# Attention and two expert layers in one kernel: K's layout and load order, and two weight preparations placed elsewhere

## The chip, the core and the metric

The kernel runs on one core of one Trainium2 chip. A core has five engines with instruction streams of their own: PE (TensorE, matmuls; its weight loads are shown apart as PEld), DVE (VectorE), ACT (ScalarE), POOL (GpSimd) and SP (SyncE, which here only issues DMAs). The metric is the device time of one execution in microseconds (us), lower is better. All times in this document are us from the start of the profiled span unless another unit is named.

## What is computed

Three stages follow each other.

- Attention for 4 batches, 8 heads, 576 positions and head size 64, in which scores more than tau below their row's maximum are dropped before the softmax:

```python
scores = scale * np.matmul(q, k.transpose(0, 1, 3, 2))
thresh = np.max(scores, axis=-1, keepdims=True) - tau
scores = np.where(scores >= thresh, scores, -1000000000.0)
attn = softmax(scores)            # out = attn @ v
```

- A feed-forward layer (FFN) on the 2304 tokens of 512 features: `h = x @ w_in` (2048 wide), a rational function P(h)/Q(h) of h with six coefficients, and the product with `w_out`.
- A layer of 8 experts of width 1024: a skip score (`x @ w_skip`) chooses the tokens, `x @ w_gate` chooses one expert for each, and `x + gate * relu(x @ w1[e]) @ w2[e]` is the output.

## The kernel before

Every float32 matrix that PE multiplies is split into a high part (the value rounded to fp32r) and a low part (the rest), and a product is three matmuls: high*high, high*low, low*high. The instruction order on every engine is the order in which the program is written (`manual_schedule`); semaphores are added for the dependences. A tile that is allocated under a tag whose buffer is still in use makes its first writer wait until the last reader of the older tile is done.

**Attention** works on 16 pairs of heads. `load(p)` (L214) issues on SP the DMAs for the K and Q of a pair, `loadv(p)` (L234) those for V. The tile `rk` has 864 columns: 288 columns with the two halves of the keys of head 0 on the partitions 0 to 63 and 64 to 127, 288 columns with the two halves of head 1 in an order that begins with its last 64 keys, and 288 columns with head 1 in its plain order. On the host, K lies as [batch, pair, head, feature, key], so `load` fills `rk` with seven DMAs of 64 partitions each; Q takes two DMAs for a pair, and eight for pair 0, which is loaded in four pieces. `high` (L246) makes the high part on ACT (for K an operation that scales in place comes first, L256, then the rounding, L257), `low` (L259) the low part: on DVE for pair 0, on POOL for the others. `smm` (L270) computes the scores on PE (L278).

A pair has nine score tiles; two of them form a unit, of which there are 72. The string SEQ (L21) writes out the order in one unit: `M` is DVE's row maximum (L284), `E` ACT's exp (L292), `A` DVE's mask with the row sum (L302), `N` PE's scores for the next unit, `t` PE's transposes, `X` and `Y` ACT's evacuations of them (L334), `V` and `W` the product with V. Each `K` takes one entry of the list `tasks`, which holds the `high` and `low` calls for the next pair (L472); each `D` moves one step of the decoding of the FFN weights (`wstep`, L425), which arrive as 64-bit floats in `raw` and are turned into high and low parts by operations on DVE, POOL and ACT (L115 to L146). Before unit 0, `load(0)`, four `wstep` calls (which issue the first load of `raw`), `load(1)` and `loadv(0)` are written, then `high`, `low` and `smm` for the first unit. Behind unit 3 the coefficients and the routing weights `wg` are loaded, ACT takes the absolute value of `cb` (L537), and DVE splits `wg` into `wgs` (L541, L542). `wgs` is first read in the FFN's second half (L702).

**FFN and experts** are one loop over steps t (from L942): 96 FFN steps (token block c of 384 tokens, slice f of the width) and then 48 expert steps (block c, slice j). In step t PE computes the first product of unit t and the second product of unit t - 3; in between, ACT, DVE and POOL apply the rational function. At the end of a step stands what the table `todo` holds for it, in the order in which the `at` calls are written. For each token block it has the reads of x2d (`pload`, L683), three steps of transposes (`tailB`, L687), the routing product and the writes of x2Td (`tailC`, L698). For the expert weights it has, with NFU = 96: `eload(j)` in step 89 + j, which issues on SP two DMAs of 256 KB into two of the four buffers `d0` to `d3`, and `esplit(j)` in step 90 + j, in which ACT makes the two high parts (L809). POOL makes the low parts (L812) in the next step, at `L` in ORD (L872). Expert slice j is first needed in step 96 + j. In step 90 POOL also issues the loads `mxs` of the first expert block (`mload`, L822), and in step 97 those of the second.

```python
def eload(e, j, tg):
    for x, src in (...):
        r = wqr[j, x] = f1.tile([P, 512], F32, tag=f"d{(2 * j + x) % 4}", ...)
        nc.sync.dma_start(r ..., src)
def esplit(j, tg, which, eng, later=True):
    nc.scalar.activation(w[:, 0], r, AF.Copy)
    def low():
        eng.tensor_tensor(w[:, 1], r, w[:, 0].bitcast(F32), op=ALU.subtract)
```

Of the kernel before, what the change touches and what calls it, by code (L numbers as in the profile page):

```python
# [9 lines left out]
F32 = mybir.dt.float32  # L10
# [3 lines left out]
AF = mybir.ActivationFunctionType  # L14
# [30 lines left out]
def body(ctx, tc, q, k, v, tau, w_in, w_out, a, b, w_skip, w_gate, w1, w2, out):  # L45
# [154 lines left out]
    with ExitStack() as actx:  # L200
# [13 lines left out]
        def load(p):  # L214
            if p >= NP:
                return
            bi, hp = divmod(p, NHP)
            rk = ap2.tile([P, NK], F32, tag="rk", name=f"rk{p}")
            rq = ap2.tile([P, NQ], F32, tag="rq", name=f"rq{p}")
            qc = ((0, NQ),) if p else ((0, 128), (704, 832), (128, 704), (832, NQ))  # L220
            for h in range(2):
                for j, h_, d0, c0, n in ((0, 0, 0, 0, 288), (1, 0, 0, 288, 288), (0, 1, 288, 512, 64), (0, 1, 352, 0, 224),
                                         (1, 1, 288, 224, 288), (0, 1, 576, 0, 288), (1, 1, 576, 288, 288)):
                    if h == h_:
                        nc.sync.dma_start(rk[64 * j:64 * j + 64, d0:d0 + n], k[bi, hp, h, :, c0:c0 + n])  # L225
                for c0, c1 in qc[h:h + 1]:
                    for j in range(2):
                        nc.sync.dma_start(rq[64 * j:64 * j + 64, c0:c1], q[bi, hp, :, c0:c1])
            for c0, c1 in qc[2:]:
                for j in range(2):  # L230
                    nc.sync.dma_start(rq[64 * j:64 * j + 64, c0:c1], q[bi, hp, :, c0:c1])
            raws[p] = rk, rq
# [12 lines left out]

        def high(p, i, c0, c1):  # L246
            if p >= NP:
                return
            if (p, i) not in qks:
                qks[p, i] = ap2.tile([P, 2, (NK, NQ)[i]], F32R, tag="KQ"[i], name=f"{'KQ'[i]}{p}")  # L250
            o, x = qks[p, i][:, 0, c0:c1], raws[p][i][:, c0:c1]
            if i == 0 and p == 0:
                nc.scalar.activation(o, x, AF.Copy, scale=scq)
                return
            if i == 0:
                nc.scalar.activation(x, x, AF.Copy, scale=scq)  # L256
            nc.scalar.activation(o, x, AF.Copy)  # L257

        def low(p, i, c0, c1):  # L259
            if p >= NP:  # L260
                return
            t = qks[p, i][:, :, c0:c1]
            x = raws[p][i][:, c0:c1]
            if i == 0 and p == 0:
                nc.vector.scalar_tensor_tensor(t[:, 1], x, scq, t[:, 0].bitcast(F32), op0=ALU.mult, op1=ALU.subtract)
                return
            eng = nc.vector if p == 0 else nc.gpsimd
            eng.tensor_tensor(t[:, 1], x, t[:, 0].bitcast(F32), op=ALU.subtract)  # L268
# [166 lines left out]
        nc.sync.dma_start(taub, tau.partition_broadcast(P))  # L435
        load(0)
        for _ in range(4):
            wstep()
        load(1)
        loadv(0)  # L440
        nc.vector.tensor_scalar(scq, taub, 0.0, -1.0 / math.sqrt(D), op0=ALU.is_ge, op1=ALU.mult)
        nc.vector.tensor_scalar(ptau, taub, 0.0, None, op0=ALU.max)
        for h in range(2):
            ks = (0, 0, 288) if h == 0 else (0, 288, NK)
            qs = (1, 704 * h, 704 * h + 128)
            for x in (ks, qs):
                high(0, *x)
            for x in (ks, qs):
                low(0, *x)
            smm(0, 0, h)  # L450
# [11 lines left out]
        for i in range(NS // 2 + 2):  # L462
# [4 lines left out]
            for x in cur:  # L467
                if x[1:] == (0, 0):
                    load(x[0] + 2)
                    n = x[0] + 1  # L470
                    z = ((0, 0, 432), (0, 432, NK), (1, 0, 608), (1, 608, NQ))
                    tasks += [[(high, n, *z[0])], [], [(high, n, *z[1])], [(low, n, *z[0])], [(high, n, *z[2])],  # L472
                              [(low, n, *z[1])], [(high, n, *z[3])], [(low, n, *z[2]), (low, n, *z[3])]]
                elif x[1:] == (2, 0):
                    loadv(x[0] + 1)
# [58 lines left out]
            if i == 3:  # L534
                nc.sync.dma_start(ca, a.partition_broadcast(P))
                nc.sync.dma_start(cb, b.partition_broadcast(P))
                nc.scalar.activation(cb, cb, AF.Abs)  # L537
                nc.vector.memset(cc, 1.0 + 1e-6)
                nc.sync.dma_start(wg[:, :, 0:E], w_gate.rearrange("(k p) e -> p k e", p=P))
                nc.sync.dma_start(wg[:, :, E], w_skip.rearrange("(k p) -> p k", p=P))  # L540
                nc.vector.tensor_copy(wgs[:, :, 0, :], wg)  # L541
                nc.vector.tensor_tensor(wgs[:, :, 1, :], wg, wgs[:, :, 0, :].bitcast(F32), op=ALU.subtract)  # L542
            if i in XS:
# [9 lines left out]
            if 70 <= i < 70 + min(XN, 2):  # L553
                xget(i - 70)
        sctx.close()
        psH = ctx.enter_context(tc.tile_pool(name="psH", bufs=4, space=PSUM, reuse_waits="tile"))
# [365 lines left out]
    for j in range(NF2):  # L922
        at(NFU - 7 + j, lambda j=j: eload(G["e"], j, "s"))
        for x in range(2):
            at(NFU - 6 + j, esplit, j, "s", x, nc.gpsimd)
    at(NFU - 6, mload, 0, "s")
# [114 lines left out]
```

## Time and profile before

| | |
|---|---|
| Runs | 985.34, 982.91, 985.03 us; median 985.03 |
| The profiled execution | 985.22 us, of which the span of the profile is 983.4 |
| PE, PEld | 913.0 us busy (93%), 749.5 (76%) |
| DVE, ACT, POOL | 701.1 (71%), 618.1 (63%), 483.3 (49%) |
| DMA | 124.15 MB, mean 126 GB/s |

How to read it: the profile is one execution. A busy time is the union of an engine's instructions, as a share of the span. An engine works its instructions in order, so one that waits holds up all that stand behind it on that engine. In a timeline, each row gives start, duration, engine, line, operation, the tile written and the tiles read, the shape, the count of merged instructions, and in brackets the engine's idle time ahead of it with what ended it. "SPq" and "POOLq" rows are the issuing of DMAs, not their transfer. PEclk is the clock granted to PE as a part of full speed. Attention fills about the first 325 us, the FFN follows up to 761 us, the experts stand behind it.

### The profile page before, as it was taken

The numbers are of one execution on the slowest core, as the hardware profiler recorded it, in microseconds if no ns is written. First come the engines' busy times: TensorE is split into PE (matmuls) and PEld (weight loads), VectorE is DVE, ScalarE is ACT, GpSimd is POOL, SyncE is SP. The second block draws the span as 40 slices with busy tenths as digits, with TensorE's granted clock in tenths as the row PEclk, the third lists the DMA queues.
The fourth block names the chain that finished last, engine by engine and source line by source line (L and its number), as shares of the span: only waits on it lengthen the run. The fifth ranks groups of instructions, "written<-read, shape, count | busy, mean of one in ns | idle before, by whom it ended". The sixth has DMA issues, their size and how long they took to land.

```text
span 983.4 us, 15831 instructions
## 1 busy us (share of the span) xinstructions
PE 913.0 (93%) x5442; PEld 749.5 (76%) x5442; DVE 701.1 (71%) x1450; ACT 618.1 (63%) x1153; POOL 483.3 (49%) x484
## 2 busy tenths in 40 slices
PE   3899889988899999999999999999998999999995
PEld 2666556656566799778888898888887988989884
DVE  4999999997988599888999877877875442221211
ACT  4798788887787688777787877777767311111110
POOL 1567569777883276998976733333346400000000
PEclk9999999999999999999999999999998999999998
DMA  5536446564644132244442332532527633122111
GB/s 151 130 96 172 117 138 180 153 194 123 179 134 173 56 107 91 87 156 153 150 160 74 129 107 86 182 118 88 186 80 238 212 129 128 65 98 95 65 33 35
DMA packets 74406, 124.15 MB, mean 126 GB/s; under 512 B 15184, under 2 KB 51536, under 8 KB 74320
## 3 DMA queue, kind: packets, MB, share of 16 engines
q1 hardware_dynamic: 70000, 99.48, 32.7%
q0 software_dynamic: 4320, 23.59, 6.9%
q8 instruction: 45, 0.74, 0.3%
q14 instruction: 41, 0.34, 0.1%
HBM read 85.22 MB, written 37.82 MB: 125 GB/s over the span
## 4 chain that ended last, share of the span: by engine, by line
PE 62%; DVE 15%; ACT 6%; POOL 6%; issue 5%; DMA 3%; SPq 3%; POOLq 0%; DVEq 0%; ACTq 0%
PE acc L604 14%; PE h L190 14%; PE mhs L190 10%; PE Ys L604 10%; PE S L278 4%; DVE m L284 3%; PE O L356 3%; PE T L314 3%; DVE P L302 2%; DMA rq<-in_q_dram 1%; ACT P L292 1%; SPq L225 1%; POOL Q L268 1%; DVE p L633 1%; DVE t L115 1%
## 5 line engine op out<-in xcount | busy, mean ns | idle before, releaser
L604 PE MATMUL acc<-wo,g 128*128 128x512 f32 x864 | 223.7, 401 | 9.6 <-ACT g L654 7.1
L604 PEld LDWEIGHTS acc<-wo,g 128*128 128x128 f32 x864 | 159.7, 190 | 49.8 <-ACT g L654 11.7
L623 POOL TENSOR_TENSOR qd<-v,qd 128x384 f32<-128x384 f32 x96 | 98.5, 1026 | 167.2 <-ACT v L620 166.1
L190 PE MATMUL h<-xg,wi 128*128 128x384 f32 x864 | 166.7, 342 | 0.0
L190 PEld LDWEIGHTS h<-xg,wi 128*128 128x128 f32 x864 | 153.5, 190 | 4.9 <-issue 0.5
L278 PE MATMUL S<-K,Q 64*128 64x288 f32 x960 | 97.2, 323 | 47.9 <-DVE P L302 36.5
L278 PEld LDWEIGHTS S<-K,Q 64*128 64x128 f32 x960 | 72.1, 191 | 88.9 <-issue 50.2
L850 DVE SCALAR_TENSOR_TENSOR mgs<-mhs,mgs 128x384 fp32r<-128x384 f32 x48 | 26.8, 558 | 151.1 <-ACT mgs L849 151.1
L292 ACT ACTIVATE P<-S,m 128x576 f32<-128x576 f32 x144 | 102.2, 741 | 47.4 <-DVE m L284 45.9
L849 ACT ACTIVATE mgs<-mhs 128x384 fp32r<-128x384 f32 x48 | 23.6, 492 | 169.8 <-PE Ys L604 168.6
L302 DVE SCALAR_TENSOR_TENSOR P<-S,m,P 128x576 f32<-128x576 f32 x144 | 111.4, 810 | 9.8 <-ACT P L292 9.8
L284 DVE TENSOR_REDUCE m<-S 128x1 f32<-128x576 f32 x144 | 103.5, 751 | 16.8 <-PE S L278 15.0
L190 PE MATMUL mhs<-mxs,wss 128*128 128x384 f32 x576 | 109.1, 337 | 0.0
L604 PE MATMUL Ys<-wss,mgs 128*128 128x512 f32 x432 | 108.5, 396 | 0.0
L190 PEld LDWEIGHTS mhs<-mxs,wss 128*128 128x128 f32 x576 | 101.6, 188 | 4.0
L604 PEld LDWEIGHTS Ys<-wss,mgs 128*128 128x128 f32 x432 | 80.1, 188 | 16.1
L628 DVE TENSOR_TENSOR p<-p,h 128x384 f32<-128x384 f32 x96 | 52.7, 549 | 47.5 <-ACT p L622 45.4
L314 PE MATMUL T<-idn,P 128*128 128x128 f32 x576 | 86.2, 291 | 0.0
L356 PE MATMUL O<-PT,V 128*64 128x320 f32 (+1 forms) x512 | 78.1, 426 | 0.6 <-ACT xT L369 0.6
L314 PEld LDWEIGHTS T<-idn,P 128*128 128x128 f32 x576 | 66.0, 147 | 12.6 <-issue 10.9
L616 ACT ACTIVATE qd<-h 128x384 f32<-128x384 f32 x96 | 46.6, 485 | 45.4 <-PE h L190 45.2
L334 ACT ACTIVATE PT<-T 128x512 f32<-128x512 f32 x128 | 71.2, 600 | 0.5 <-PE T L314 0.5
(149 smaller groups left out, 1538.7 us busy)
## 6 DMA issues: line engine op xcount, KB each, us to landing
xg<-xSd POOLq DMA_DIRECT2D x18, 768.0 KB, 5.7
x2Td<-x2h SPq DMA_DIRECT2D x12, 768.0 KB, 4.4
mxs<-x2Td POOLq DMA_DIRECT2D x12, 768.0 KB, 5.6
rq<-in_q_dram SPq DMA_DIRECT2D x30, 304.0 KB, 4.2
raw<-in_moe_w_in_dram SPq DMA_DIRECT2D x16, 512.0 KB, 4.2
raw<-in_moe_w_out_dram SPq DMA_DIRECT2D x16, 512.0 KB, 3.8
rk<-in_k_dram SPq DMA_DIRECT2D x80, 72.0 KB, 2.9
xSd<-px SPq DMA_DIRECT2D x24, 192.0 KB, 2.0
```

Source lines behind the costliest of these rows:

```text
L190: nc.tensor.matmul(h, w[:, sw, 128 * k:128 * k + 128], x[:, sx, k], start=(k == 0 and i == 0), stop=(k == NKT - 1 and i == 2))
L278: nc.tensor.matmul(st[:, c, :288], Q[d, x, q0:q0 + P], K[d, y, k0:k0 + 288], start=(s == 0 and j in (0, h)), stop=(s == 2 and (r < 4 or j ...
L284: nc.vector.tensor_reduce(m[:, 0:1], st, axis=AX.XY, op=ALU.min)
L292: nc.scalar.activation(e, st, AF.Exp, bias=m[:, 0:1], scale=-1.0)
L302: nc.vector.scalar_tensor_tensor(e, st, m[:, 1:2], e, op0=ALU.is_le, op1=ALU.mult, accum_out=sums[:, bi, col, hp:hp + 1])
L314: nc.tensor.transpose(T[:, 128 * j:128 * j + 128], pt[:, j0:j0 + 128], idn)
L334: nc.scalar.activation(dst[:, 5 * h:5 * h + 4, c0:c0 + 128], T.rearrange("p (j c) -> p j c", c=128), AF.Copy)
L356: nc.tensor.matmul(o[d, :w], vts[p][:, x, j, :], pt[:, j + 5 * x, :], start=(j == 0), stop=False)
L604: nc.tensor.matmul(ac[t], g[:, sg, 128 * t:128 * t + 128], w[:, sw, :], start=(first and i == 0), stop=(last and i == 2))
L616: nc.scalar.activation(u, h, AF.Abs)
L623: nc.gpsimd.tensor_tensor(qd, v, u, op=ALU.mult)
L628: nc.vector.tensor_tensor(p, p, hs[c, f], op=ALU.mult)
```

## The change

It has three parts.

1. The host lays K out as [batch, pair, 128, 576]: rows are the two key halves times 64 features, and columns are the two heads, 288 each, with head 1 in the order that begins with its last 64 keys. `load` then fills the first 576 columns of `rk` with one DMA of 128 partitions (two for pair 0), and the last 288 columns with three DMAs behind those of Q. Pair 0's K and Q pieces are issued in the order in which they are used, `load(1)` is written ahead of the first `wstep` calls, and only the first two K pieces and the first two Q pieces of pair 0 go through ACT and DVE ahead of unit 0. The large Q pieces get their low parts on POOL, and the last K piece becomes a task of unit 0, with its low part on POOL; the tasks of pair 1 move back by up to one unit.
2. The split of `wg` into `wgs` moves from behind unit 3 to behind the last unit of attention. The absolute value of `cb` moves from behind unit 3 to behind unit 10.
3. `esplit(j)` moves from step 90 + j to step 92 + j; `eload(j)` stays.

```diff
+            kd, qd = k[bi, hp], q[bi, hp]
+            kc = ((0, 576),) if p else ((0, 288), (288, 576))
             qc = ((0, NQ),) if p else ((0, 128), (704, 832), (128, 704), (832, NQ))
-            for h in range(2):
-                for j, h_, d0, c0, n in ((0, 0, 0, 0, 288), (1, 0, 0, 288, 288), (0, 1, 288, 512, 64), (0, 1, 352, 0, 224),
-                                         (1, 1, 288, 224, 288), (0, 1, 576, 0, 288), (1, 1, 576, 288, 288)):
-                    if h == h_:
-                        nc.sync.dma_start(rk[64 * j:64 * j + 64, d0:d0 + n], k[bi, hp, h, :, c0:c0 + n])
-                for c0, c1 in qc[h:h + 1]:
-                    for j in range(2):
-                        nc.sync.dma_start(rq[64 * j:64 * j + 64, c0:c1], q[bi, hp, :, c0:c1])
-            for c0, c1 in qc[2:]:
+            for i in range(len(qc)):
+                for c0, c1 in kc[i:i + 1]:
+                    nc.sync.dma_start(rk[:, c0:c1], kd[:, c0:c1])
                 for j in range(2):
-                    nc.sync.dma_start(rq[64 * j:64 * j + 64, c0:c1], q[bi, hp, :, c0:c1])
+                    nc.sync.dma_start(rq[64 * j:64 * j + 64, qc[i][0]:qc[i][1]], qd[:, qc[i][0]:qc[i][1]])
+            for r0, c0, r1, c1 in ((slice(0, P), slice(576, 800), slice(0, P), slice(352, 576)),
+                                   (slice(0, 64), slice(800, 864), slice(64, P), slice(288, 352)),
+                                   (slice(64, P), slice(800, 864), slice(0, 64), slice(288, 352))):
+                nc.sync.dma_start(rk[r0, c0], kd[r1, c1])
...
-            eng = nc.vector if p == 0 else nc.gpsimd
+            eng = nc.vector if first else nc.gpsimd
...
         load(0)
+        load(1)
         for _ in range(4):
             wstep()
-        load(1)
...
         for h in range(2):
-            ks = (0, 0, 288) if h == 0 else (0, 288, NK)
+            ks = (0, 288 * h, 288 * h + 288)
             qs = (1, 704 * h, 704 * h + 128)
             for x in (ks, qs):
-                high(0, *x)
+                high(0, *x, True)
             for x in (ks, qs):
-                low(0, *x)
+                low(0, *x, True)
...
-                    tasks += [[(high, n, *z[0])], [], [(high, n, *z[1])], [(low, n, *z[0])], [(high, n, *z[2])],
-                              [(low, n, *z[1])], [(high, n, *z[3])], [(low, n, *z[2]), (low, n, *z[3])]]
+                    hi, lo = [(high, n, *x) for x in z], [(low, n, *x) for x in z]
+                    if n == 1:
+                        tasks += [[], [(high, 0, 0, 576, NK), (low, 0, 0, 576, NK)], [hi[0]], [hi[1]], [lo[0], hi[2]], [lo[1]], [hi[3]], [lo[2], lo[3]]]
+                    else:
+                        tasks += [[hi[0]], [], [hi[1]], [lo[0]], [hi[2]], [lo[1]], [hi[3]], [lo[2], lo[3]]]
...
             if i == 3:
...
-                nc.scalar.activation(cb, cb, AF.Abs)
...
-                nc.vector.tensor_copy(wgs[:, :, 0, :], wg)
-                nc.vector.tensor_tensor(wgs[:, :, 1, :], wg, wgs[:, :, 0, :].bitcast(F32), op=ALU.subtract)
+            if i == 10:
+                nc.scalar.activation(cb, cb, AF.Abs)
...
+        nc.vector.tensor_copy(wgs[:, :, 0, :], wg)
+        nc.vector.tensor_tensor(wgs[:, :, 1, :], wg, wgs[:, :, 0, :].bitcast(F32), op=ALU.subtract)
         sctx.close()
...
-            at(NFU - 6 + j, esplit, j, "s", x, nc.gpsimd)
+            at(NFU - 4 + j, esplit, j, "s", x, nc.gpsimd)
...
-                x = y
+                y[:, :, 1] = _np.roll(y[:, :, 1], S - n, axis=3)
+                x = y.reshape(B, H // 2, 2, D, 2, S // 2).transpose(0, 1, 4, 3, 2, 5).reshape(B, H // 2, 2 * D, S)
```

## Rows read from the trace of the kernel before

**Rows 1.** Busy us (instructions) by stretch, granted PE clock, DMA share and GB/s

```profile
core 0: us, PE busy (x) PEld busy (x) DVE busy (x) ACT busy (x) POOL busy (x), PEclk, DMA share, GB/s
100.00:150.00 50.00, 43.19 (x369) 29.38 (x371) 46.99 (x110) 40.89 (x76) 32.79 (x29) 1.00 0.43 125
...
319.00:327.00 8.00, 7.44 (x51) 4.65 (x50) 0.09 (x2) 1.92 (x5) 0.61 (x9) 1.00 0.05 16
...
736.00:742.00 6.00, 6.00 (x35) 5.51 (x33) 3.27 (x6) 1.37 (x3) 1.90 (x2) 1.00 1.07 385
742.00:746.00 4.00, 0.74 (x3) 0.46 (x2) 0.86 (x2) 3.82 (x7) 1.38 (x2) 0.82 0.35 110
746.00:750.00 4.00, 4.00 (x10) 2.58 (x10) 2.84 (x6) 3.94 (x8) 3.84 (x4) 0.50 0.21 62
```

**Rows 2.** Timeline of DVE, units 1 to 4 of attention

```profile
17.59 1.49 DVE L284 TENSOR_REDUCE m<-S 128x1 f32<-128x576 f32 x2 [0.54 <-PE S L278]
...
23.02 0.43 DVE L115 TENSOR_SCALAR t<-raw 128x512 uint32<-128x512 uint32 x1
23.64 1.50 DVE L284 TENSOR_REDUCE m<-S 128x1 f32<-128x576 f32 x2 [0.19 <-PE S L278]
...
27.95 1.42 DVE L284 TENSOR_REDUCE m<-S 128x1 f32<-128x576 f32 x2 [0.15 <-PE S L278]
...
32.16 1.17 DVE L541 CAST wgs<-wg 128x36 fp32r<-128x36 f32 x1 [0.99 <-DMA wg<-in_moe_w_skip_dram]
...
34.49 1.41 DVE L284 TENSOR_REDUCE m<-S 128x1 f32<-128x576 f32 x2
```

**Rows 3.** Timeline of ACT, the same stretch

```profile
12.82 0.52 ACT L257 ACTIVATE Q<-rq 128x384 fp32r<-128x384 f32 x1 [0.41 <-DMA rq<-in_q_dram]
14.64 1.41 ACT L292 ACTIVATE P<-S,m 128x576 f32<-128x576 f32 x2 [1.29 <-DVE m L284]
19.63 0.65 ACT L256 ACTIVATE rk<-rk,scq 128x432 f32<-128x432 f32 x1 [3.59 <-DMA rk<-in_k_dram]
...
20.79 1.36 ACT L292 ACTIVATE P<-S,m 128x576 f32<-128x576 f32 x2
22.04 1.09 ACT L334 ACTIVATE PT<-T 128x512 f32<-128x512 f32 x2
...
24.43 1.48 ACT L292 ACTIVATE P<-S,m 128x576 f32<-128x576 f32 x2 [0.18 <-DVE m L284]
...
31.70 0.67 ACT L129 ACTIVATE w<-raw 128x512 f32<-128x512 f32 x1
35.27 1.41 ACT L292 ACTIVATE P<-S,m 128x576 f32<-128x576 f32 x2 [2.90 <-DVE m L284]
```

**Rows 4.** Timeline of ACT, the split of expert piece 1

```profile
742.04 1.35 ACT L809 ACTIVATE wss<-wrs 128x512 fp32r<-128x512 f32 x2 [4.64 <-DMA wrs<-in_moe_w_dram]
```

**Rows 5.** Timeline of SP's DMA issues, the first loads

```profile
3.70 3.15 SPq L225 DMA_DIRECT2D rk<-in_k_dram  x5
...
8.17 2.51 SPq L231 DMA_DIRECT2D rq<-in_q_dram  x4
```

**Rows 6.** Timeline of POOL, a subtraction of 608 columns

```profile
31.80 1.49 POOL L268 TENSOR_TENSOR Q<-rq,Q 128x608 fp32r<-128x608 f32 x1 [2.48 <-ACT Q L257]
```

**Rows 7.** DMA issues: count, KB each, median us from issue to landing

```profile
raw<-in_moe_w_in_dram SPq DMA_DIRECT2D x16, 512.0 KB, 4.2
```

**Rows 8.** Timeline of PE, first product of steps 92, 93 and 94

```profile
735.26 2.37 PE L190 MATMUL h<-xg,wi 128*128 128x384 f32 x12
...
739.90 2.37 PE L190 MATMUL h<-xg,wi 128*128 128x384 f32 x12
...
750.54 2.74 PE L190 MATMUL h<-xg,wi 128*128 128x384 f32 x12
```

**Rows 9.** Timeline of SP, the load of expert piece 1

```profile
734.22 1.20 SPq L804 DMA_DIRECT2D wrs<-in_moe_w_dram  x2
```

**Rows 10.** The tile wrs (expert weights as loaded), time to landing

```profile
DMA to landing us min/median/max: 3.6/3.8/3.9
```

**Rows 11.** The tile wss (split expert weights): ns min/median/max, first and last start

```profile
L812 POOL TENSOR_TENSOR wss<-wrs,wss x16: 1280/1297/1330, 735.3 to 774.6; 128x512 fp32r<-128x512 f32 x16
```

More of the change, by code (lines that the diff above doesn't have):

```diff
@@ L244, in loadv, with high @@
                 nc.sync.dma_start(VZ[p % 3][d, d], v[bi, h0 + j, 512:576, :])
-        def high(p, i, c0, c1):
+        def high(p, i, c0, c1, first=False):
             if p >= NP:
@@ L251, in high @@
             o, x = qks[p, i][:, 0, c0:c1], raws[p][i][:, c0:c1]
-            if i == 0 and p == 0:
+            if i == 0 and first:
                 nc.scalar.activation(o, x, AF.Copy, scale=scq)
@@ L257, in high, with low @@
             nc.scalar.activation(o, x, AF.Copy)
-        def low(p, i, c0, c1):
+        def low(p, i, c0, c1, first=False):
             if p >= NP:
@@ L263, in low @@
             x = raws[p][i][:, c0:c1]
-            if i == 0 and p == 0:
+            if i == 0 and first:
                 nc.vector.scalar_tensor_tensor(t[:, 1], x, scq, t[:, 0].bitcast(F32), op0=ALU.mult, op1=ALU.subtract)
                 return
-            eng = nc.vector if p == 0 else nc.gpsimd
+            eng = nc.vector if first else nc.gpsimd
             eng.tensor_tensor(t[:, 1], x, t[:, 0].bitcast(F32), op=ALU.subtract)
```

## The prediction

> **What bounds the kernel now.** The engine shares come first (table above): PE is busy 93% of the span, so time is to be had only where PE idles or runs at a low clock. The busy time by stretch shows where [rows 1]. In the middle of attention (100 to 150 us) PE has 43.19 of 50 us and DVE 46.99, so DVE is the fullest engine there. Behind attention PE is nearly full, but from 742 to 746 us it has 0.74 of 4, and from 746 to 750 its granted clock is 0.50, the 1.2 GHz level. So I read the timelines, engine by engine, at the start of attention and near 742 us.
>
> In attention one unit is a ring: DVE's row maxima (L284), ACT's exps (L292), DVE's masks (L302), PE's next scores (L278), which need the score buffer that a mask frees. The maxima of units 2 and 3 start at 23.64 and 27.95 us, an undisturbed step of 4.31; from unit 1 to 2 it is 6.05 (from 17.59), and from unit 3 to 4 it is 6.54 (to 34.49) [rows 2]. In the first of these stalls ACT stood for a DMA of rk before L256, and the exps at 20.79 are queued behind that [rows 3]. In the second DVE stood for the DMA of wg before L541, and the maxima are queued behind the two wgs operations [rows 2]. Near 742 us ACT stood 4.64 us for the DMA of wrs [rows 4], with all the activations of that step queued behind it.
>
> **First loads.** SP issues one DMA in 0.63 us (five in 3.15) [rows 5]. Before, the last piece of pair 0's Q is the 15th DMA, issued at 10.09 (the last of four that begin at 8.17); ACT could use it at 12.82, 2.73 later [rows 3, 5]. Now it is the 10th, issued at 6.89, there at 9.62, and ACT's 0.52 on it ends at 10.14. The second score's K and Q pieces are issued by 4.34 and there by 7.1, so both maxima are done by 10 us. The subtractions of the large Q pieces move from DVE to POOL, where one of 608 columns takes 1.49 [rows 6]; begun at 9.2, that is over before the scores of unit 1 ask for it near 11.9, and costs nothing; begun 2 us later it would hold these scores. So exp 0 starts at 10.14 instead of 14.64.
>
> Unit 1: from exp 0 to the next maximum it took 2.95 (14.64 to 17.59), and an exp starts 0.79 behind its maximum (23.64 to 24.43) [rows 2, 3]: 13.88. Ahead of it on ACT stands now the last third of pair 0's K. Its transfers are issued up to 8.81; if they take the 4.2 us of a 512 KB one [rows 7], two operations of at most 0.52 end at 14.05. I take 14.05.
>
> Unit 2: ACT has the exps (1.41), an evacuation pair (1.09) and now both K pieces of pair 1, four operations of at most 0.65 [rows 3]: 19.2. On DVE the first weight decode (L115, 0.43) stands ahead of the maxima. Its load of raw is now the 20th DMA, since pair 1 has been moved ahead of it: issued at 13.3, there 4.2 later [rows 7], 17.5; plus 0.43, and 0.79 to the exp, 18.7 [rows 2]. ACT decides: exp 2 starts at 19.2 instead of 24.43, **5.2 us** earlier. Ends: 5.7 if exp 1 starts at 13.88 and the K operations are shorter; 4.2 if raw takes 1.5 longer because pair 1's 0.9 MB stands ahead of it.
>
> **Routing weights.** DVE is free at 31.17, waits 0.99, and has the two wgs operations till 34.49 [rows 2]. Without them its maximum is done by 31.92, and the exp is bound by ACT, which is busy till 32.37 (L129): 35.27 less 32.37, **2.9 us** [rows 3]. At most 3.3, all the time that DVE spent on it; at least 2.2, if the step becomes the undisturbed 4.31. At the new place, behind the loop, DVE is busy 0.09 us of the 8 from 319 to 327 [rows 1]: nothing, and 2.3 if that cover is gone. The Abs of cb, two columns, is put in a unit where ACT waits for DVE: nothing. The ring carries both gains to the end of attention, because DVE has the same work per unit as before. SP issues three DMAs fewer for each pair; no engine of the ring stood for SP once it ran, so this is nothing.
>
> **Expert weights.** Step 93 of the FFN loop takes from 739.90 to 750.54, 10.64 us; the step before, with the same transposes, takes 4.64 [rows 8]. The difference, **6.0 us**, is PE's wait and the low clock behind it. The cause: piece 1 of the expert's weights is issued at 734.22 and used at 742.04, 7.8 later, where a piece lands in 3.6 to 3.9 [rows 4, 9, 10]. From 736 to 742 the DMA engines are full at 385 GB/s [rows 1]: POOL's load of mxs (1.5 MB, step 90), three writes of x2d and piece 2 lie beside it. After the change piece 1 is loaded at the same time, but its split stands at the end of step 93, near 747 us, 5 us after it landed. ACT doesn't stand, PE doesn't idle, and the clock doesn't fall. At least 4.0 if a later piece makes ACT wait 2; at most 6.4, with 0.4 that step 94 also lost at the low clock by my estimate.
>
> The new wait is SP's. The four buffers hold two pieces, so the load of piece j+2 stands on SP until POOL's subtraction of piece j, which now comes two steps later. Behind it in SP's queue stand the last token block's reads of x2d (L685) and the writes of x2Td (L704). DVE's block-end sum (L674) needs the third of these reads: I get it issued near 763.5 and wanted at 768.6, and 5.1 us is more than any landing in [rows 10]. So it is just hidden; if it came later, PE would wait for DVE to free the accumulators. The pieces themselves go by hops: two subtractions of 1.30, a landing of 3.8, a split of 1.35, up to 0.6 for the order on ACT and POOL, 8.4 in all for every second piece, while PE takes two steps, 8.4 or more [rows 4, 8, 10, 11]. Piece 1 is done near 754.6 and piece 7 three hops later at 779.8; the expert stage starts at 754.7 and asks for piece 7 after seven steps of 4.2, at 784. Nothing, with 4 us to spare.
>
> Of the landing, the rows show 7.8 once, beside mxs, and at most 3.9 in the rest [rows 4, 9, 10]. The Trainium skill (DMA: Bandwidth & Descriptors, Issuing engines are not separate DMA queues) says that DMAs started by different engines run on the same 16 DMA engines and interleave; the trace agrees with 385 GB/s. By that rule the second load of mxs, which POOL issues in step 97, would stretch one more hop from 8.4 to 12.4 and use up the 4 us to spare, which speaks for the third rival below; by the bare rows the hop stays 8.4. The sum is the same by both.
>
> **Sum.** 5.2 + 2.9 + 6.0 = 14.1, from the profiled execution's 985.22 us (a span of 983.4 and 1.8 around it): 971.1. The median of the runs, 985.03, lies 0.2 under that execution.
>
> **Rivals.** (1) The splits stand later, but the wait returns at piece 2 or 3, because their loads start two steps later too, so the change doesn't do what it says. Then the third term is gone: 985.2 - 8.1 = 977.1. For it: a hop of 8.4 is no shorter than two steps. Against: the first round has 5 us of air, and no 1.5 MB load lies beside pieces 2 and 3. Chance 0.12. (2) The ring wins back late time anyway, and the start's gain is lost on the way. Only the 6.0 remains: 979.2. For it: DVE idles 3 us of 50, room in which 8 us of delay could be made up over 300 us. Against: those idle moments are the ring's own waits, and the two stalls came from outside it [rows 1, 2]. Chance 0.10. (3) Slower: the hops get long, and PE waits for pieces in its first eight expert steps. Three hops have 29.4 us (754.6 to 784), 9.8 each, which a landing of 5.2 fills. Each us more per landing costs 3, and a stall brings some 2.5 at the low clock, so 14.1 is eaten from a landing of about 9. At 10 it is 3 x 4.8 + 2.5 - 14.1, 2.8 over: 988. For it: 7.8 was seen once. Against: it needs more than that three times over. Chance 0.03.
>
> **Numbers.** The forecast has 0.75. With the ends of its terms the gain is 10.4 to 15.4, which is 969.8 to 974.8; the lowest run shown is 2.1 under the median, so I set the low end at 967.5. The high end takes in the first two rivals: 979.5. About 0.3% (3 us) is what a measurement of this kernel can tell from no change. The forecast and the first two rivals are all faster by more than that, 0.97; 0.02 of it I give to the case that both of these hold in part, which is the same; slower 0.03.
>
> **What would show it.** Right: exp 2 near 19 us; no DVE wait for wg and an even step from unit 3 to 4; the end of attention about 8 us earlier; no PE gap near 735 us and a clock of 1.00 there; the expert stage beginning 14 us earlier. Wrong: ACT waiting for wrs at a later piece; PE waiting for wss; L674 waiting for a read of x2d; late exps back at their old times.

## The result, and the profile after

The changed kernel takes 972.16 us (median of 972.53, 972.6, 968.34 and 971.8), the kernel before on the same chip 984.55: ratio 0.9868, 95% interval 0.9839 to 0.9896. That is 12.4 us less, 1.1 from the 971.1 predicted. Taken again later beside other kernels, the same kernel gave 970.27 and the same ratio, 0.9868 (0.9847 to 0.9888). The profiled execution took 972.53, a span of 970.6.

To see where the time went I use one measure throughout, the **lead**: by how much the same work starts earlier than in the profile of before, taken at the first row maximum (L284) of an attention unit and at the first product (L190) of a step. For the changed kernel it is 4.2 us at unit 2, 4.7 at unit 4, 5.6 at the last unit, 5.8 at step 93, and 12.1 from step 95 to the end. So the time was won in two places, the first units and step 93 to 94, and between units 2 and 4, where 2.9 was predicted, hardly any came.

The expert weights first: PE's products and ACT's splits around the place where ACT stood 4.64 us in [rows 4]. (In the changed kernel the split of L809 is L813.)

```profile
729.51 2.37 PE L190 MATMUL h<-xg,wi 128*128 128x384 f32 x12
...
734.15 2.37 PE L190 MATMUL h<-xg,wi 128*128 128x384 f32 x12
...
738.79 2.36 PE L190 MATMUL h<-xg,wi 128*128 128x384 f32 x12
```

```profile
736.03 1.14 ACT L813 ACTIVATE wss<-wrs 128x512 fp32r<-128x512 f32 x2
...
740.68 1.14 ACT L813 ACTIVATE wss<-wrs 128x512 fp32r<-128x512 f32 x2
...
745.80 0.63 ACT L813 ACTIVATE wss<-wrs 128x512 fp32r<-128x512 f32 x1 [0.30 <-DMA wrs<-in_moe_w_dram]
```

Step 93 takes 738.79 - 734.15 = 4.64 instead of the 10.64 of [rows 8], and no split of the first two pieces waits. The windows there show a full PE at clock 1.00, where [rows 1] has 0.74 of 4 and then 0.50:

```profile
core 0: us, PE busy (x) PEld busy (x) DVE busy (x) ACT busy (x) POOL busy (x), PEclk, DMA share, GB/s
...
728.00:734.00 6.00, 6.00 (x33) 5.30 (x32) 5.36 (x11) 4.85 (x9) 1.78 (x2) 1.00 0.97 342
734.00:740.00 6.00, 6.00 (x36) 5.56 (x35) 4.53 (x10) 5.84 (x12) 2.89 (x4) 1.00 0.36 124
```

Now the start of attention. These are ACT's rows of the changed kernel; the exps (L292) of units 0 to 2 answer to those of [rows 3]:

```profile
9.64 1.35 ACT L292 ACTIVATE P<-S,m 128x576 f32<-128x576 f32 x2
...
13.29 1.48 ACT L292 ACTIVATE P<-S,m 128x576 f32<-128x576 f32 x2 [1.40 <-DVE m L284]
...
20.19 1.41 ACT L292 ACTIVATE P<-S,m 128x576 f32<-128x576 f32 x2 [2.16 <-DVE m L284]
```

Exps 0 and 1 are a little ahead of the 10.14 and 14.05 predicted. Exp 2 is 1.0 behind its 19.2, and its bracket names a cause that the prediction had ruled out: ACT was idle 2.16 us and waited for DVE. DVE's rows and PE's say why:

```profile
12.50 1.50 DVE L284 TENSOR_REDUCE m<-S 128x1 f32<-128x576 f32 x2 [0.53 <-PE S L278]
...
18.51 0.98 DVE L115 TENSOR_SCALAR t<-raw 128x512 uint32<-128x512 uint32 x1 [2.72 <-DMA raw<-in_moe_w_in_dram]
19.41 1.41 DVE L284 TENSOR_REDUCE m<-S 128x1 f32<-128x576 f32 x2
...
29.79 1.42 DVE L284 TENSOR_REDUCE m<-S 128x1 f32<-128x576 f32 x2 [2.82 <-PE S L278]
```

```profile
22.55 1.83 PE L278 MATMUL S<-K,Q 64*128 64x288 f32 x12 [4.71 <-DVE P L302]
```

The first decode of an FFN weight (L115) stood 2.72 us on DVE for `raw`, whose load is now issued behind those of pair 1; unit 2's maxima are queued behind it. So DVE's masks came late, and PE stood 4.71 us for them. After that PE ran at a lower granted clock:

```profile
core 0: us, PE busy (x) PEld busy (x) DVE busy (x) ACT busy (x) POOL busy (x), PEclk, DMA share, GB/s
16.00:20.00 4.00, 1.84 (x16) 1.43 (x16) 1.49 (x2) 1.97 (x4) 2.89 (x3) 1.00 1.08 277
20.00:24.00 4.00, 1.45 (x12) 1.48 (x12) 3.81 (x11) 3.25 (x6) 0.48 (x1) 0.69 0.76 170
24.00:28.00 4.00, 4.00 (x22) 2.63 (x21) 2.97 (x9) 3.53 (x6) 1.40 (x2) 0.50 0.77 202
28.00:32.00 4.00, 4.00 (x40) 2.77 (x36) 1.83 (x5) 1.49 (x4) 3.59 (x3) 0.96 0.43 117
```

From 24 to 28 us PE is busy throughout at 0.50, the 1.2 GHz level, and does 22 matmuls where it does 40 in the next four. It is the bound there, and DVE, now without the two `wgs` operations, waits 2.82 us for PE's scores ahead of unit 4's maxima (29.79). My theory from this: one late load at the start both delayed exp 2 and lowered the clock, and the slow PE swallowed what the routing weights should have given. The rival: the three parts' gains are simply smaller than thought, each by itself.

### The profile page after: what moved, and what is told of

It reads as the page before. It is cut to its first block, busy times and chain, and to the rows that moved or that the text cites. A ratio compares the mean times of both kernels' runs of the same rounds, so it can differ in the third digit from the quotient of the medians.

```text
span 970.6 us, 15750 instructions
## 1 busy us (share of the span) xinstructions
PE 908.5 (94%) x5442; PEld 747.8 (77%) x5442; DVE 696.7 (72%) x1448; ACT 618.9 (64%) x1155; POOL 485.5 (50%) x487
## 4 chain that ended last, share of the span: by engine, by line
PE 65%; DVE 15%; ACT 6%; POOL 6%; issue 5%; SPq 1%; DMA 1%; POOLq 0%; DVEq 0%; ACTq 0%
PE acc L608 15%; PE h L190 15%; PE mhs L190 10%; PE Ys L608 10%; PE S L278 5%; DVE m L284 4%; PE O L356 4%; PE T L314 3%; DVE P L302 3%; ACT P L292 1%; DVE t L115 1%; DVE p L637 1%; DVE h L652 1%; DVE raw L117 1%; DVE h L650 1%
## 5 line engine op out<-in xcount | busy, mean ns | idle before, releaser
L608 PE MATMUL acc<-wo,g 128*128 128x512 f32 x864 | 221.1, 398 | 6.2 <-ACT g L658 3.7
L190 PE MATMUL h<-xg,wi 128*128 128x384 f32 x864 | 166.6, 342 | 0.0
L190 PEld LDWEIGHTS h<-xg,wi 128*128 128x128 f32 x864 | 153.5, 190 | 4.9 <-issue 0.5
L292 ACT ACTIVATE P<-S,m 128x576 f32<-128x576 f32 x144 | 102.5, 741 | 48.4 <-DVE m L284 47.3
L284 DVE TENSOR_REDUCE m<-S 128x1 f32<-128x576 f32 x144 | 103.7, 751 | 19.4 <-PE S L278 17.5
L190 PE MATMUL mhs<-mxs,wss 128*128 128x384 f32 x576 | 109.2, 338 | 0.0
L190 PEld LDWEIGHTS mhs<-mxs,wss 128*128 128x128 f32 x576 | 101.7, 188 | 4.0
L268 POOL TENSOR_TENSOR Q<-rq,Q 128x608 fp32r<-128x608 f32 (+2 forms) x32 | 47.6, 1490 | 56.4 <-ACT Q L257 56.2
```

Of the source, the lines that this page charges most:

```text
L190: nc.tensor.matmul(h, w[:, sw, 128 * k:128 * k + 128], x[:, sx, k], start=(k == 0 and i == 0), stop=(k == NKT - 1 and i == 2))
L284: nc.vector.tensor_reduce(m[:, 0:1], st, axis=AX.XY, op=ALU.min)
L292: nc.scalar.activation(e, st, AF.Exp, bias=m[:, 0:1], scale=-1.0)
L608: nc.tensor.matmul(ac[t], g[:, sg, 128 * t:128 * t + 128], w[:, sw, :], start=(first and i == 0), stop=(last and i == 2))
```

## Experiments

All kernels were timed beside the kernel before, which took 983.98 us beside the first four of them, 984.52 beside the next four and 984.33 beside the last four.

**The parts, one at a time.** Each of these three kernels is the kernel before with one part of the change:

```diff
 p1_loads: part 1 (K's layout, load order, first parts)
 p2_wg:    part 2 (split of wg behind attention, Abs of cb behind unit 10)
 p3_split: part 3
-            at(NFU - 6 + j, esplit, j, "s", x, nc.gpsimd)
+            at(NFU - 4 + j, esplit, j, "s", x, nc.gpsimd)
```

> Part 1 alone (K's layout, load order, pair 1 ahead of raw; wgs and the expert splits where they were). Theory (DVE stands for raw at unit 2, PE idles and then runs at the low clock into unit 4): maxima of unit 2 start near 19.4 us as in the changed kernel, 4.2 earlier than before; at unit 4 DVE still has to split wg, whose loads land near 28.4, so its maxima start near 31 us; the total is 3.5 to 4.5 us below the kernel before, about 980.5. Rival (the terms of the start are independent and only smaller than forecast): 5 us below, about 979.5.

> Part 2 alone (wgs behind attention, Abs of cb behind unit 10). Theory (in the changed kernel PE's low clock hid this term): alone it gives what the rows of before said, maxima of unit 4 near 31.6 instead of 34.49 us, a total 2.5 to 3 us below the kernel before, about 982. Rival (the ring wins the time back in the next units): under 1 us, about 984.

> Part 3 alone (splits of the expert weights two steps later). Theory: the 6.3 us by which the changed kernel's step 93 is shorter are this part's alone: about 978.2, no PE gap and a clock of 1.00 in steps 92 to 95. Rival (the gap is missing in the changed kernel because the start moved the loop against the DMA traffic): the gap stays and the total is within 1 us of before.

| kernel | median us (all runs) | ratio (95%) | gain, us |
|---|---|---|---|
| p1_loads | 977.54 (976.35 to 978.76) | 0.9936 (0.9922 to 0.9949) | 6.4 |
| p2_wg | 980.95 (978.08 to 983.47) | 0.9965 (0.9953 to 0.9976) | 3.0 |
| p3_split | 976.92 (975.25 to 978.44) | 0.9925 (0.9911 to 0.994) | 7.1 |

Alone the parts give 16.5 us, together 12.4 (14.1 in the second measurement). The rival is out: part 2 alone gives 3.0 us, and in its profile the lead grows from 0.5 at unit 3 to 2.9 at unit 4, the place where the two `wgs` operations stood.

Not all of the difference between 16.5 and 12.4 comes from the parts, though. In step 88 of the FFN loop, which no part touches, PE has the same 1.40 us of idle in all 14 profiles. In ten of them its clock then falls, and the step takes 5.8 us; in four (p1_loads, p2_wg, qlow_dve, split_plus4) it doesn't, and the step takes 4.28. The windows of that step, first of before, then of p1_loads:

```profile
716.00:720.00 4.00, 3.70 (x15) 3.70 (x16) 2.21 (x7) 0.04 (x1) 0.00 (x0) 0.65 0.00 0
711.00:715.00 4.00, 3.44 (x19) 3.26 (x20) 2.47 (x7) 1.06 (x3) 0.00 (x0) 1.00 0.00 0
```

So 1.5 us of what the profiles of p1_loads and p2_wg gain on that of before is none of the parts' doing. How much of this is in the medians, no run shows.

Part 1 alone gave more than I expected. In its profile the lead is 4.6 at the last unit, and 1.5 in step 88 and 0.8 in step 93 come on top. Attention itself was ahead of the expectation too: the maxima of unit 2 start at 18.36 instead of near 19.4. Its maxima of unit 4 I had put near 31 us, with the stall for `wg` still in front; DVE's rows of p1_loads show them at 29.30, ahead even of the changed kernel's 29.79:

```profile
18.02 0.43 DVE L115 TENSOR_SCALAR t<-raw 128x512 uint32<-128x512 uint32 x1 [2.20 <-DMA raw<-in_moe_w_in_dram]
...
27.20 0.92 DVE L544 CAST wgs<-wg 128x36 fp32r<-128x36 f32 x1 [1.24 <-DMA wg<-in_moe_w_skip_dram]
28.15 1.22 DVE L545 TENSOR_TENSOR wgs<-wg,wgs 128x36 fp32r<-128x36 f32 x1
29.30 1.41 DVE L284 TENSOR_REDUCE m<-S 128x1 f32<-128x576 f32 x2
```

The two `wgs` operations with their wait fill time in which DVE would otherwise stand for the slow PE, whose clock here was 0.57 and 0.58 from 20 to 28 us. There they cost little, so taking them away gives little.

**raw ahead of pair 1.** The changed kernel with the late load alone put back in its place:

```diff
         load(0)
-        load(1)
         for _ in range(4):
             wstep()
+        load(1)
         loadv(0)
```

> The changed kernel with the first load of raw issued ahead of pair 1 again (one line moved back). Theory: L115 finds raw landed, no wait of DVE before it; maxima of unit 2 start near 17.5 us, PE idles under 3 us there and keeps a clock of 1.00 from 20 to 28 us, maxima of unit 4 near 26.5 us; total 3 us below the changed kernel, about 969. Rival (pair 1 now lands 0.6 us later and ACT stands for it instead; or the low clock comes from the light load at the start in any case): within 1 us of the changed kernel, about 972.

It takes 968.26 us (966.95 to 969.17), ratio 0.9841 (0.9826 to 0.9855): 3.9 less than the changed kernel, 2.9 less than the median of all eight runs of it (971.2), and 2.7 less by the two ratios. The intervals overlap, so the size is rough. DVE's and PE's rows of raw_first:

```profile
15.71 0.42 DVE L115 TENSOR_SCALAR t<-raw 128x512 uint32<-128x512 uint32 x1
16.32 1.46 DVE L284 TENSOR_REDUCE m<-S 128x1 f32<-128x576 f32 x2 [0.19 <-PE S L278]
...
26.41 1.42 DVE L284 TENSOR_REDUCE m<-S 128x1 f32<-128x576 f32 x2 [1.65 <-PE S L278]
```

```profile
20.34 1.83 PE L278 MATMUL S<-K,Q 64*128 64x288 f32 x12 [2.10 <-DVE P L302]
```

L115 has no wait, the exp of unit 2 starts at 18.61, and the leads are 7.3 at unit 2, 8.1 at unit 4 and 10.0 at the last unit. PE still stood 2.10 us, and the clock from 20 to 24 us was 0.57, not the 1.00 I had expected: part of the loss is left. In the changed kernel's second profile (changed_again, below) the leads are 5.3, 6.8 and 8.8, so raw_first is ahead of both profiles at each of these places.

**Part 2 with and without the late load.** If the slow PE hides part 2, undoing part 2 must cost little in the changed kernel and more in raw_first. In both, the Abs and the two `wgs` operations go back behind unit 3:

```diff
             if i == 3:
...
+                nc.scalar.activation(cb, cb, AF.Abs)
...
+                nc.vector.tensor_copy(wgs[:, :, 0, :], wg)
+                nc.vector.tensor_tensor(wgs[:, :, 1, :], wg, wgs[:, :, 0, :].bitcast(F32), op=ALU.subtract)
-            if i == 10:
-                nc.scalar.activation(cb, cb, AF.Abs)
...
-        nc.vector.tensor_copy(wgs[:, :, 0, :], wg)
-        nc.vector.tensor_tensor(wgs[:, :, 1, :], wg, wgs[:, :, 0, :].bitcast(F32), op=ALU.subtract)
```

> The changed kernel without part 2 (wgs and the Abs of cb back behind unit 3). Theory: in the changed kernel DVE stands 2.8 us for scores at unit 4 that PE makes at the low clock, and the two wgs operations fit into that wait, so taking part 2 away costs 0 to 1 us: about 972.5. Rival (part 2 earns its 2.9 us here too): about 975.

> The kernel with raw ahead of pair 1, without part 2. Theory: where PE's scores come earlier, the wgs operations stand in the way again: maxima of unit 4 near 28.6 instead of 26.4 us, total about 970.4, 2.2 us over raw_first (968.3). Rival (part 2 is worth nothing once part 1 is there): 968.3.

no_p2 takes 972.76 (972.13 to 973.76), ratio 0.9888 (0.987 to 0.9905); raw_first_no_p2 970.44 (969.73 to 971.71), ratio 0.9859 (0.9839 to 0.9879). Part 2 is thus worth 972.76 - 972.16 = 0.6 us behind the late load (1.6 against all eight runs) and 970.44 - 968.26 = 2.2 without it. The direction is as the theory has it, but the intervals overlap, so the medians alone would not show it. The lead around the place, beside PE's granted clock, says more:

| profile | lead at units 2, 3, 4 | from 3 to 4 | clock, 20 to 24 and 24 to 28 us |
|---|---|---|---|
| changed kernel, first | 4.2, 4.3, 4.7 | 0.4 | 0.69, 0.50 |
| changed_again | 5.3, 5.3, 6.8 | 1.5 | 0.70, 0.87 |
| raw_first | 7.3, 6.5, 8.1 | 1.6 | 0.57, 1.00 |
| raw_first_hi1 (below) | 7.3, 7.6, 10.1 | 2.5 | 1.00, 1.00 |
| qlow_dve (below) | 5.8, 5.9, 8.4 | 2.5 | 1.00, 1.00 |
| p2_wg | 0.5, 0.5, 2.9 | 2.5 | 0.72, 1.00 (24 to 28, 28 to 32) |
| p1_loads, without part 2 | 5.3, 5.3, 5.2 | -0.1 | 0.57, 0.58 |
| no_p2, without part 2 | 5.4, 5.4, 5.3 | -0.1 | 0.66, 0.91 |
| raw_first_no_p2, without part 2 | 7.6, 6.8, 6.5 | -0.3 | 0.68, 0.89 |

With part 2 the lead grows by 2.5 where PE had its full clock between units 3 and 4, by 1.5 and 1.6 where the clock was lower for a part of that time, and by 0.4 where it was 0.50; without part 2 it doesn't grow. So the slow PE hides 1 to 2 of the 2.5 us, and not always all of it: changed_again and no_p2 start alike and differ by 1.5 at unit 4. The leads at the last unit are a poor measure of part 2. Those of the changed kernel's first profile and no_p2 are nearly equal (5.6 and 5.7), but that profile had lost 1.1 more at unit 2; and of the 10.0 of raw_first against the 6.6 of raw_first_no_p2, 1.4 arise behind unit 50, where none of these edits stands.

**Waiting for raw later.** The same late load, with the first decode steps written later in the units:

```diff
-PACE_A = (8, 1, 1, 1, 1, 3, 2, 1, 3)
+PACE_A = (10, 1, 1, 1, 1, 3, 2, 1, 3)
```

> The changed kernel with its load order kept, but every weight decode begun two of its moves later, so that L115 of the first stands in unit 3 and not in unit 2. Theory (it is DVE's stand for raw, not the load order as such, that costs): no wait before L115, maxima of unit 2 near 16.5 us, no low clock of 8 us behind it, total within 1 us of raw_first, about 968.5. Rival (pair 1 ahead of raw costs by the DMA queue, whoever waits): about 972.

The start is as expected. DVE and the window of pace:

```profile
20.22 0.42 DVE L115 TENSOR_SCALAR t<-raw 128x512 uint32<-128x512 uint32 x1
...
26.10 1.41 DVE L284 TENSOR_REDUCE m<-S 128x1 f32<-128x576 f32 x2
```

```profile
24.00:28.00 4.00, 3.50 (x34) 2.60 (x34) 3.76 (x10) 1.44 (x3) 3.43 (x3) 1.00 0.80 222
```

No wait, clock 1.00, a lead of 8.4 at unit 4. But the time is 973.03 (970.98 to 973.33), ratio 0.9879 (0.9861 to 0.9898), no better than the changed kernel and near the rival's number, although the start is the theory's: the lead wanders between 1.6 and 8.9 from unit 6 to 60 and is 4.7 at the last unit. The edit also shifts where every later decode step falls in the units, and what it won at the start was lost again there. At which instruction stays open.

**Splits two steps later still.** Is part 3 near an edge, and is it the pieces' or SP's?

```diff
 (on top of raw_first)
-            at(NFU - 4 + j, esplit, j, "s", x, nc.gpsimd)
+            at(NFU - 2 + j, esplit, j, "s", x, nc.gpsimd)
```

> The kernel with raw ahead of pair 1 and the splits of the expert weights four steps later than before instead of two. Theory (a piece is worth two steps of delay, with 4 to 6 us to spare in the hops): piece 0 has its low part some 2.5 us after step 96 asks for it, and the next pieces follow by hops of 8.4 us, so PE stands for wss in steps 96 to 100 and falls to the low clock: 6 to 12 us over raw_first, 974 to 980. Rival (the ordering on SP has plenty of room): within 1 us of raw_first, 968.3.

It takes 983.06 us (978.39 to 985.95), ratio 0.9981 (0.9966 to 0.9996): 14.8 more than raw_first, beyond the expectation. The lead falls from 15.8 at step 95 to 3.4 at step 100 and 1.4 at step 140. PE's, DVE's, POOL's and SP's rows of split_plus4 (the rows of POOL and SP are issues):

```profile
746.76 2.02 PE L190 MATMUL mhs<-mxs,wss 128*128 128x384 f32 x10 [0.75 <-POOL wss L816]
...
752.70 2.01 PE L190 MATMUL mhs<-mxs,wss 128*128 128x384 f32 x10 [1.51 <-POOL wss L816]
...
770.53 1.65 PE L608 MATMUL Ys<-wss,mgs 128*128 128x512 f32 x3 [6.74 <-DVE x L678]
```

```profile
769.78 0.69 DVE L678 SCALAR_TENSOR_TENSOR x<-acc,x 128x512 f32<-128x512 f32 x1 [7.07 <-DMA x<-x2d]
```

```profile
756.33 1.12 POOL L831 DMA_DIRECT2D mxs<-x2Td  x2
```

```profile
756.80 0.91 SPq L708 DMA_DIRECT2D x2Td<-x2h  x2
757.75 0.43 SPq L689 DMA_DIRECT2D x<-x2d  x1
759.32 1.81 SPq L808 DMA_DIRECT2D wrs<-in_moe_w_dram  x2
761.24 0.40 SPq L689 DMA_DIRECT2D x<-x2d  x1
```

PE waits for pieces, but only 0.75 and 1.51. The large stall begins where the prediction looked for one, in SP's queue: the expert loads stand there for a free buffer, and reads of x2d are queued behind them. DVE's block-end sum (L678, L674 before) stands 7.07 us for one of these reads, and PE 6.74 for the accumulator that this sum frees. But the late issue is only part of it. This read was issued at 757.75, 5.0 us before DVE wanted it (769.78 less 7.07), and used 12.0 after its issue; the next, issued at 761.24, was used at 772.06, 10.8 after. Ahead of both stands POOL's second load of `mxs`, 1.5 MB, issued at 756.33; in raw_first the last of these reads is issued at 752.77, ahead of that load (754.63). So the wait on SP moved the reads behind a large load, and their landing took longer than the prediction allowed for. How much either does by itself, no run shows.

**Splits one step earlier.** The other side of the same edit, again on raw_first: `NFU - 5 + j`.

> The kernel with raw ahead of pair 1 and the splits of the expert weights one step later than before instead of two. Theory (7.8 us of landing against a step of 4.6): piece 1, issued near 724, lands near 732, when its split is due; ACT stands under 1 us and PE not at all: within 0.5 us of raw_first, 968.3. Rival (one step does not cover the landing, and PE falls to the low clock as before): 3 us or more over raw_first, 971 to 974.

969.06 us (965.28 to 969.69), ratio 0.9834 (0.9813 to 0.9855), the same as raw_first, and ACT's rows show no wait at the first pieces (727.95 and 732.64). One step later than before is enough; two cost nothing.

**The changed kernel again**, to see how far its start varies:

> The changed kernel once more, on the same chip and beside the same runs of before as the next three. Expected 972 with a spread of some 4 us. If the low clock at the start is what separates its quick runs (968.3) from the others (972.5), a profile in a quick run shows 1.00 from 20 to 28 us, and one of a usual run shows 0.5 to 0.7 there.

970.27 us (969.37, 970.58, 973.22, 969.97). The profile is of the quickest of these four, and it doesn't have the clean start I looked for: L115 stood 2.13 us (0.44 long, not 0.98), exp 2 came at 19.14, and the windows have

```profile
20.00:24.00 4.00, 2.46 (x16) 2.21 (x17) 3.83 (x9) 2.96 (x6) 1.59 (x2) 0.70 0.95 222
24.00:28.00 4.00, 4.00 (x37) 2.88 (x36) 2.26 (x9) 3.03 (x6) 1.42 (x1) 0.87 0.60 149
```

so 37 matmuls against 22 in the second stretch, and a lead of 6.8 at unit 4 against 4.7. That the quickest run, 968.34, had a clock of 1.00 throughout is thus not shown; that some of the spread arises in this stretch is.

**The second K piece of pair 1 one slot later.** In raw_first, ACT scales and rounds both K pieces of pair 1 ahead of exp 2. With the second behind it:

```diff
 (on top of raw_first)
-                        tasks += [..., [hi[0]], [hi[1]], [lo[0], hi[2]], [lo[1]], [hi[3]], ...]
+                        tasks += [..., [hi[0]], [], [lo[0], hi[1]], [hi[2], lo[1]], [hi[3]], ...]
```

> The kernel with raw ahead of pair 1, and the second K piece of pair 1 made in unit 2 instead of unit 1. Theory (what is left at the start is ACT, which makes two K pieces in unit 1 and stands 0.57 us for the second): exp 2 starts near 17.6 instead of 18.6 us, PE idles 1 us less behind it and keeps the full clock, the maxima of unit 4 start near 24.9 instead of 26.4 us; total 1 to 1.5 us under raw_first, about 967. Rival (the work is only moved, and ACT holds unit 3 up instead): 968.3.

967.63 us (966.12 to 968.83), ratio 0.9829 (0.9813 to 0.9845), the lowest median of all: 16.7 under the kernel before and 2.6 under the changed kernel timed beside it (970.27). The 0.6 that it is under raw_first is less than a measurement can tell. Its start is clean. ACT, PE and the windows of raw_first_hi1:

```profile
17.13 1.41 ACT L292 ACTIVATE P<-S,m 128x576 f32<-128x576 f32 x2 [0.23 <-DVE m L284]
```

```profile
19.52 1.40 PE L278 MATMUL S<-K,Q 64*128 64x288 f32 x12 [1.30 <-DVE P L302]
```

```profile
20.00:24.00 4.00, 3.92 (x40) 2.78 (x38) 3.59 (x12) 3.97 (x8) 2.83 (x3) 1.00 0.95 195
24.00:28.00 4.00, 3.55 (x34) 2.39 (x31) 3.20 (x8) 3.70 (x8) 3.92 (x4) 1.00 0.78 195
```

PE stands 1.30 us, its clock stays at 1.00, and the lead at unit 4 is 10.1.

**The large Q pieces' low parts back on DVE** tests the one move inside part 1 that the prediction had costed at nothing:

```diff
 (on top of raw_first)
-            low(0, *x)
+            low(0, *x, True)
```

> The kernel with raw ahead of pair 1 and the low parts of pair 0's large Q pieces on DVE, as before the change. Theory (exp 0 is set by ACT's last Q piece at 9.7 us, not by DVE): DVE makes them at 8.9 and 9.8 us, its first mask starts at 10.4 as in raw_first, and the total stays within 0.5 us of raw_first, 968.3. Rival (POOL's part is what frees the ring's start): exp 0 or the first mask 0.5 to 1 us later and the total as much higher.

968.74 us (968.35 to 970.79), ratio 0.9849 (0.9833 to 0.9865). DVE's rows:

```profile
8.87 0.76 DVE L268 TENSOR_TENSOR Q<-rq,Q 128x576 fp32r<-128x576 f32 x1 [1.97 <-ACT Q L257]
9.79 0.56 DVE L268 TENSOR_TENSOR Q<-rq,Q 128x384 fp32r<-128x384 f32 x1 [0.16 <-ACT Q L257]
10.26 1.42 DVE L284 TENSOR_REDUCE m<-S 128x1 f32<-128x576 f32 x2
```

The maxima of unit 0 stand behind the subtractions and their wait, so the lead at unit 0 is 3.6 instead of 7.1, and the first mask starts at 11.90, later than I had put it. Yet the time is as in raw_first: unit 4 has a lead of 8.4, since PE here stood 1.17 us instead of 2.10 and kept its clock. The 3.5 us lost at unit 0 were made up by unit 4. At the last unit, though, the lead is 8.0 against 10.0, and 1.5 of that comes back in step 88, which was short in this profile: that the totals are equal is in part chance.

## Why the prediction was right, and the step of it that failed

- **Total and direction** held: 972.16 against 971.1, within the range.
- **First loads, exps 0 and 1** held (9.64 and 13.29 for 10.14 and 14.05). The last third of pair 0's K was ready by 11.90 and no longer bound exp 1.
- **First loads, exp 2: the step that failed.** The prediction put `raw` "there 4.2 later", at 17.5, and let ACT decide, busy till 19.2. `raw` was there 6.0 later (issued at 12.54, used at 18.51), and ACT was done with its K pieces at 18.03. So DVE decided, exp 2 came at 20.19, and the term gave 4.2 instead of 5.2; the lower end of the term allowed just that ("4.2 if raw takes 1.5 longer"). In the other three profiles with this load order (p1_loads, no_p2, changed_again) `raw` was used 5.4 to 5.5 after its issue, DVE decided again, and exp 2 came at 19.06 to 19.14. There the number 5.2 fits, but by luck: ACT was faster than the working had it and `raw` slower. DVE's decode took 0.98 in the first profile and 0.43 or 0.44 in the other three. In the first it began (18.51) inside POOL's second subtraction of a K piece (18.11 to 19.20) and ended 0.28 behind it; in the other three it began in the last 0.16 us of the first subtraction, and the second then took 1.20 to 1.26 instead of 1.09. The Trainium skill (SBUF — State Buffer, SBUF: two separate sides) says that DVE and GpSimd share a pair of ports which one instruction holds to its end, while the other's stands, if DVE's runs in a two-port mode or reads two inputs from SBUF; the rows fit that, but no row shows in which mode L115 ran, and no run took the subtraction away alone.
- **Routing weights: the mechanism was right, its size was not, in this company.** Alone the part gives 3.0 in time and 2.5 in the lead, against the 2.9 predicted. Behind the late load it gave 0.5 from unit 2 to 4 (4.2 to 4.7), 1.5 in the second profile. What the working left out is that the stall ahead of exp 2 is also PE's, 4.71 us, and that PE works at half clock behind it: then PE, and not only DVE, sets unit 4. The table of leads above shows it. The new place is free, as said: the two operations take 0.18 and 0.20 us there.
- **The ring carries the gains**: the lead didn't fall (4.7 at unit 4, 5.6 at the last).
- **Expert weights** held: the lead grows by 6.4 from step 93 to 95, against 6.0 and an estimate of 0.4 behind it; p3_split gives the same 6.4. ACT waits for later pieces up to 4.37 us, and PE for none: that sign was listed as one against the forecast, and it wasn't, because those splits had the time.
- **SP's new wait** held: the third read of x2d is issued at 758.34 and used near 764.1, 5.8 for the 5.1 of the working. But the reason given, that this is more than any landing, was thin: in split_plus4 such reads took 10.8 and 12.0.
- **The signs** held in part. DVE didn't wait for `wg`, and the gap of PE near 735 us is gone. But the step from unit 3 to 4 is not even: it takes 29.79 - 23.67 = 6.12 us, little less than the 6.54 before. Attention ends 5.6 us earlier, not 8 (8.8 in the second profile), and the expert stage begins 12.1 earlier, not 14 (15.4 in the second).
- **Why the sum came near all the same:** the lead of 12.1 is 4.2 + 0.5 + 6.4, 0.9 that grew between unit 4 and the last unit, and 0.2 up to step 93, each rounded. A term too large by 1.0 and one by 2.4 met one too small by 0.4 and drift that I had put at nothing. And the forecast set out from 985.22, 0.7 above the 984.55 of the comparison. So the mechanism of the third term was right, and the nearness of the total is in part luck.
- **The rivals.** The wait at piece 2 or 3 (977.1) didn't come: 0.30 us on ACT at piece 2. The ring didn't win back the start (979.2). The slow side (988) did not come here; split_plus4 reached 983.06, mainly by the late reads of x2d and less by the waits for pieces that this rival priced, but beside the same second load of `mxs`. What did come was none of the three: a new wait at the start that took back much of one term.

## What to carry to other kernels

Order the first loads by who stands for them in program order on the fullest engine, not by which stage they belong to: `raw` belongs to the FFN, but its decode stood ahead of attention's maxima. Before adding two gains on one chain, ask which engine sets the place of the second once the first is made; gains of 6.4, 3.0 and 7.1 gave 12.4. Before reading a difference of 1 or 2 us, look at a place that the change doesn't touch: step 88 alone differed by 1.5. A load that waits for a buffer on an in-order queue must be priced by what stands behind it in that queue, by who waits for that, and by which large loads it then falls behind.

## What the runs showed of the hardware that was not expected

- Short idle times of PE differ in what follows. In step 88, 1.40 us of idle was followed by a lower clock in ten profiles and by none in four. At the start of attention, 4.71 us was followed by 0.69 and 0.50 in the next two stretches, 3.20 (p1_loads) by 0.57 and 0.58, 3.62 (changed_again) by 0.70 and 0.87, and 2.10 by 0.57 and 1.00; 1.30 and 1.17 were not followed by a fall.
- The load of `raw` took 6.0 us from issue to use with pair 1's transfers ahead of it, and 5.4 to 5.5 in the other three profiles with this order, where [rows 7] has 4.2.
- The two operations on 36 columns of `wgs` took 0.92 and 1.22 us in attention (p1_loads), where each ended 0.04 to 0.05 us behind the POOL subtraction that was running when it began (to 28.08 and 29.32):

```profile
26.59 1.49 POOL L268 TENSOR_TENSOR Q<-rq,Q 128x608 fp32r<-128x608 f32 x1 [2.63 <-ACT Q L257]
28.03 1.30 POOL L126 TENSOR_TENSOR lf<-lf,t 128x512 f32<-128x512 f32 x1
```

  The same holds for both in before and no_p2. In raw_first_no_p2 the second of them began together with a subtraction of POOL (27.88), and took 0.20. Behind attention, where POOL has nothing beside them, they take 0.18 and 0.20:

```profile
L557 DVE CAST wgs<-wg x1: 183/183/183, 312.8 to 312.8; 128x36 fp32r<-128x36 f32 x1
L558 DVE TENSOR_TENSOR wgs<-wg,wgs x1: 197/197/197, 313.0 to 313.0; 128x36 fp32r<-128x36 f32 x1
```
